# Two linear-attention layers on one core: the attention-output matrix from split factors in three float32r passes

## Chip, cores, metric

The kernel runs on one core of a Trainium2 chip. The metric is the device time of one execution in microseconds, as the median of several runs. One further execution was recorded by the hardware profiler; all lines of the trace come from it.

## What is computed

Two pairs of a linear-attention block A and a feed-forward block B, with the same weights in both pairs, on x of 2048 rows and 640 columns (32 heads of 20 columns, 1728 hidden units), all in float32:

```python
def _A_ref(x, wqkv, wo):
    qkv = (x @ wqkv).reshape(B, S, 3, H, Dh).transpose(2, 0, 3, 1, 4)
    q, k, v = qkv[0], qkv[1], qkv[2]
    phi = lambda t: jnp.where(t > 0, t + 1, jnp.exp(t)) + 1e-6
    pq, pk = phi(q), phi(k)
    kv = jnp.einsum("bhsd,bhse->bhde", pk, v)
    z = jnp.einsum("bhsd->bhd", pk)
    num = jnp.einsum("bhqd,bhde->bhqe", pq, kv)
    den = jnp.einsum("bhqd,bhd->bhq", pq, z)[..., None] + 1e-6
    return (num / den).transpose(0, 2, 1, 3).reshape(B, S, D) @ wo

def _B_ref(x, w1, b1, w2, b2):
    r = relu(einsum("bsd,df->bsf", x, w1) + b1)
    return einsum("bsf,fd->bsd", r * r, w2) + b2

x = x + _A_ref(_layernorm(x), A_wqkv, A_wo)
x = x + _B_ref(_layernorm(x), B_w1, B_b1, B_w2, B_b2)
...                                   # and both once more
```

## The kernel before

The 2048 rows are 16 tiles of 128 (`NT`), in four groups of four (`TG`). Large products are made in float32r, a form of float32 that TensorE takes in one pass with fewer bits. To keep the precision, each operand is split into a high part (a copy rounded to float32r, by ACT) and a low part (the operand minus the high part, by VectorE), and a product is the sum of three passes: low x high, high x low, high x high (`split`, `mm3`).

**Phase A, the loop over t.** For each tile, K and Q are projected (`part`), phi is applied (`Phi`: an exponential on ACT, L616, then two VectorE operations, L623 and L624), and x and phi(k) are split (`xh`, L925 and L955; `kh`, L810 and L820 in `k_post`). The products x^T phi(k) of the previous tile go into five PSUM banks (`g_part`, G) and, for pairs of tiles, into GT (`gt_part`). The sum of phi(k) over tiles is kept in `acc`: GpSimd adds the tiles with accumulating DMAs, and the last tile with an addition (L817). The q parts of six tiles in each layer are "late" (`LATE`): they are made after the loop by `late_q`, one half tile each.

**Between A and B.** This is the stretch that the change touches, in the order of the code:

1. Two late q parts (`late_q(2)`). Then a matrix of ones times `acc` sums phi(k) over the partitions, in two float32 matmuls of 320 columns (L1030); ACT copies it to `zbc`, with which VectorE makes the denominators (`b_ops`, walked through by `b_step`, `b_den`, `b_blocks`).
2. The last `g_part` and `gt_part`, and a transposition of GT into `Gs`.
3. `kv_make(c)` for six chunks of six heads (120 rows, the last one 40): G times the v weights, masked by VectorE to the block diagonal `kvbd` (L1084). v weights were loaded by `load_vo(0..2)`.
4. `m_make(c)` for the six chunks: kvbd times the rows of wo that belong to these heads, two float32 matmuls of 320 columns (L1093). The product, evicted by ACT (L1099) and moved into place by DMAs (L1103, L1105), is the attention-output matrix M, of 640 x 640; `m_split` splits its five chunks (L1108, L1109). The attention of a tile is then phi(q) / den times M: no per-head product is left.
5. The first products with M (`proj`, L538), for tiles 0 to 3, and the residual sums and norms that follow (`b_x1`); `b_load_x` loads x for them. Between all these steps `run_side` lets ACT move 32 x 32 blocks (L475) for transposed tiles.

The rest is the feed-forward block (`fc1`, `fc2_step`), with the attention of later groups woven in; the change does not touch it.

**Order and waits.** The order of instructions on each engine is the order in the code; each engine, and each DMA queue, takes them one after the other and waits at an instruction whose operands or whose tile aren't free. Tiles come from tagged rings: `f` (8 tiles of 128 x 640), `g` (5), `u` (6 tiles of twice that size), `r` (3, only for phase A). A new tile takes the buffer that was given up first, and its first writer waits for the last reader of the buffer. The loads of wo are issued by SyncE in the last two iterations of the loop:

```python
        if t >= 13:
            b_load_pq(t - 13)
            load_vo(2 * t - 26)
            load_vo(2 * t - 25)
```

PSUM has eight banks. `xbank` hands out banks 0, 1, 2 in turn, `kv_make` takes 3, 4, 5, 6, 7, 2, and `m_make` pairs from 4, 6, 2.

Of the kernel before, what the change touches and what calls it, by code (L numbers as in the profile page):

```python
# [31 lines left out]
HR = 6 * DH  # L32
# [21 lines left out]
F_BUFS, X_BUFS = 8, 5  # L54
# [14 lines left out]
def head_rows(c):  # L69
    return min(HR, D - HR * c)  # L70
# [3 lines left out]
def kernel(  # L74
# [11 lines left out]
    nc = tc.nc  # L86
# [5 lines left out]
    tmp = ctx.enter_context(tc.tile_pool(name="tmp", bufs=3))  # L92
# [26 lines left out]
    def ftile(name):  # L119
        return tmp.tile([P, D], F32, tag="f", name=name, bufs=F_BUFS)  # L120

    def gtile(name):
        return tmp.tile([P, D], F32, tag="g", name=name, bufs=X_BUFS)


    def split(hi, lo, src):

        nc.scalar.activation(hi, src, AF.Copy)
        nc.vector.tensor_tensor(out=lo, in0=src, in1=hi.bitcast(F32), op=ALU.subtract)
# [24 lines left out]
    def utile(name):  # L154
        return tmp.tile([P, 2 * D], R32, tag="u", name=name, bufs=RING)
# [86 lines left out]
    for m in ORDER:  # L242
        for k in range(PAIRS):
            a, b = unit_range(k)
# [310 lines left out]
    def a_stats(t):  # L555
        if t < NT:
            ln_stats(("a", t), xt[t])
# [12 lines left out]
    for layer in range(N_LAYERS):  # L570
# [57 lines left out]
        def rtile():  # L628
            return ap.tile([P, D], F32, tag="r", name="r", bufs=3)
# [28 lines left out]
        if layer == 0:  # L658
# [38 lines left out]
            first_loads.step(1, 5)  # L697
            first_loads.high(1)
            first_loads.low(1)
        ones = ap.tile([P, P], F32, name="ones", tag="ones", bufs=1)  # L700
        nc.gpsimd.memset(ones, 1.0)
        mask = ap.tile([HR, 6, DH], F32, name="mask", tag="mask", bufs=1)
        nc.gpsimd.memset(mask, 1.0)

# [9 lines left out]
        vo = {}  # L714

        def load_vo(i):

            u = utile("uraw").bitcast(F32).rearrange("p (j n) -> p j n", j=2)
            for j in range(2):
                c = 2 * (i % 3) + j  # L720
                if i < 3 and c < DC:
                    nc.sync.dma_start(u[:, j], wqkv[c * P : (c + 1) * P, 2 * D :])
                if i >= 3:
                    n = head_rows(c)
                    nc.sync.dma_start(u[:n, j], wo[c * HR : c * HR + n, :])
                vo["v" if i < 3 else "o", c] = u[:, j]

        pq, xr, pT, yzp, yzx, xn = {}, {}, {}, {}, {}, {}
        dens, xTb = {}, {}
# [15 lines left out]
        def b_load_x(t):  # L745
            xr[t] = x1_at(t)
            nc.sync.dma_start(xr[t], src[t])
# [59 lines left out]
        def k_post(t, r, between=()):  # L807

            kh[t] = u = xtile("kh")
            nc.scalar.activation(u[:, 0], r, AF.Copy)  # L810
            if t == 0:
                nc.gpsimd.tensor_copy(acc, r)
            else:
                if t < NT - 1:
                    nc.gpsimd.dma_start(acc, r, accum_op=ALU.add)
                else:
                    nc.gpsimd.tensor_tensor(out=acc, in0=acc, in1=r, op=ALU.add)  # L817
            for f in between:
                f()
            nc.vector.tensor_tensor(out=u[:, 1], in0=r, in1=u[:, 0].bitcast(F32), op=ALU.subtract)  # L820
# [32 lines left out]
        for t in range(NT):  # L853
# [117 lines left out]
            else:  # L971
                ps = part(t, 1024, 2 * D, bank(xb[2]))
                gs(1)
            k_post(t, f.r, [lambda: a_stats(t + 3)])
            if gt and not is_late:
                gt_part(t // 2 - 1, 1, bank(xb[1]))
            prep_step(t, 3)
# [43 lines left out]
        def run_keep(n):  # L1021
            for _ in range(min(n, len(keeps))):
                keep_kq(*keeps.pop(0))

        run_keep(2)
        late_q(2)
        zbc = tmp.tile([P, D], F32, tag="z", name="zbc", bufs=1)
        psz = [xbank()[:, :HD] for _ in range(2)]
        for j in range(2):
            nc.tensor.matmul(psz[j], ones, acc[:, j * HD : (j + 1) * HD], start=True, stop=True)  # L1030
        for j in range(2):
            nc.scalar.activation(zbc[:, j * HD : (j + 1) * HD], psz[j], AF.Copy)
        b_den(0)
# [32 lines left out]
        u = xtile("kvbd", F32).rearrange("p j n -> p (j n)")  # L1066
        kvbd = [u[:, HR * c : HR * (c + 1)] for c in range(NH)]
        maskf = mask.rearrange("p h d -> p (h d)")
        kvb = [3, 4, 5, 6, 7, 2]

        def kv_make(c):
            n = head_rows(c)
            kvb.append(kvb.pop(0))
            ps = bank(kvb[-1])

            o, m = HR * c, max(min(DM - HR * c, n), 0)
            parts = [v for v in ((0, m, G, o), (m, n, Gs, max(o - DM, 0))) if v[0] < v[1]]
            for q0, q1, g, w0 in parts:
                for d in range(DC):
                    nc.tensor.matmul(  # L1080
                        ps[:n, q0:q1], vo["v", d][:, o : o + n],
                        g[:, d, w0 : w0 + q1 - q0], start=d == 0, stop=d == DC - 1,
                    )
            nc.vector.tensor_tensor(out=kvbd[c][:n, :n], in0=ps[:n, :n], in1=maskf[:n, :n], op=ALU.mult)  # L1084

        mb = [4, 6, 2]

        def m_make(c):
            mb.append(mb.pop(0))
            ps = bank(mb[-1], 2)  # L1090
            n, o = head_rows(c), HR * c
            for j in range(2):
                nc.tensor.matmul(  # L1093
                    ps[:n, j * 512 : j * 512 + HD], kvbd[c][:n, :n],
                    vo["o", c][:n, j * HD : (j + 1) * HD], start=True, stop=True,
                )

            u = m_raw[0] if c == 0 else ftile("Mc")
            nc.scalar.activation(halves_sb(u[:n]), halves(ps[:n]), AF.Copy)  # L1099
            if c > 0:  # L1100
                m, r = divmod(o, P)
                k = min(P - r, n)
                nc.sync.dma_start(m_raw[m][r : r + k], u[:k])  # L1103
                if k < n:
                    nc.sync.dma_start(m_raw[m + 1][: n - k], u[k:n])  # L1105
# [7 lines left out]
        for c in range(NH):  # L1113
            kv_make(c)
            if c == 0:
                b_load_pq(3)
            if c == 1:
                b_load_x(0)
            if c == 3:
                b_load_x(1)  # L1120
            if c == 2:
                run_side(1)
            if c < 3:
                b_step(2)
        sg.close()
        sm = ExitStack()
# [10 lines left out]
        xbanks = [0, 1]  # L1137
        for c in range(NH):
            m_make(c)
            run_side(1)  # L1140
            b_step(3)
            if c == 2:
                late_q(1)
            if c in (3, 4):
                m_split(c - 3)
# [649 lines left out]
```

## Time and profile before

| | |
|---|---|
| median of 3 runs | 1312.54 us (1312.44 to 1313.02) |
| the profiled execution | 1313.91 us |
| its span, first to last instruction | 1312.2 us |
| granted TensorE clock | 1.0 |
| PE / VectorE / ACT / GpSimd busy | 1305.5 / 924.0 / 743.6 / 238.0 us |
| bytes moved | 339.94 MB, mean 259 GB/s |

Engines are called PE (TensorE matmuls), PEld (its weight loads), DVE (VectorE), ACT (ScalarE), POOL (GpSimd) and SP (SyncE, which issues most DMAs); a q behind the name is the engine's queue of DMA issues and waits. In a line of the timeline, the start (us from the start of the span) comes first, then the length of the burst, the engine, the line of the code, the operation, output <- inputs, shapes, and the number of instructions; in brackets at its end stands the engine's idle time before it and what ended that. In a line of groups the total busy time and the mean of one (ns) stand behind the bar. A profile that shows PE busy all the time says that PE never ran out of matmuls, not that each was fast.

### The profile page before, as it was taken

Reading aid. Unit: us, or ns where it says so; the run is one execution under the profiler, and the core shown is the slowest. Engines: PE = TensorE matmul, PEld = TensorE weight load, DVE = VectorE, ACT = ScalarE, POOL = GpSimd, SP = SyncE. Lnnn points to the kernel's source line nnn. Section 1 sums busy time; section 2 is a strip of 40 time slices with the busy share of each in tenths; the row PEclk is TensorE's granted clock in tenths of the full one; section 3 lists DMA queues with packets and bytes.
Section 4 is the critical chain, followed back from the end, with each engine's and each line's share of the span. In section 5 each row is a group of like instructions: output and inputs, shape, how many; then the busy total and the mean of one; then the engine's idle time right before and its main releaser. Section 6 shows DMA issues by size and latency. Waiting matters only on the chain.

```text
span 1312.2 us, 21124 instructions
## 1 busy us (share of the span) xinstructions
PE 1305.5 (99%) x7441; PEld 1187.8 (91%) x7441; DVE 924.0 (70%) x1697; ACT 743.6 (57%) x1636; POOL 238.0 (18%) x305
## 2 busy tenths in 40 slices
PE   9999999999999999999999999999999999999998
PEld 8888889989988988998988889999899899889888
DVE  7888978767865965833856677587779479579145
ACT  5888957785385476334322233387755934944242
POOL 2334310064032102101012222102330030021000
PEclk9999999999999999999999999999999999999999
DMA  6888985699996996998954456544879779779756
GB/s 194 249 278 268 310 256 167 248 353 386 304 342 207 307 344 231 290 369 293 354 173 125 126 141 170 146 175 169 328 275 372 274 257 326 294 253 313 288 187 221
DMA packets 143071, 339.94 MB, mean 259 GB/s; under 512 B 17318, under 2 KB 67622, under 8 KB 142326
## 3 DMA queue, kind: packets, MB, share of 16 engines
q1 hardware_dynamic: 135734, 316.31, 70.5%
q0 software_dynamic: 7232, 22.29, 6.6%
q8 instruction: 59, 0.97, 0.3%
q14 instruction: 46, 0.38, 0.1%
HBM read 255.92 MB, written 70.78 MB: 249 GB/s over the span
## 4 chain that ended last, share of the span: by engine, by line
PE 92%; DMA 3%; DVE 3%; SPq 1%; ACT 0%; issue 0%; POOL 0%; ACTq 0%; DVEq 0%
PE PS L1245 28%; PE PS L1328 24%; PE PS L603 18%; PE PS L511 11%; PE PS L1539 4%; PE PS L538 3%; PE PS L652 2%; DMA u<-kept 2%; PE PS L1080 1%; PE PS L1093 1%; DMA kept<-uprep 1%; PE PS L876 0%; DMA st<-in_B_w_dram 0%; DMA st<-in_A_wqkv_dram 0%; DVE uprep L332 0%
## 5 line engine op out<-in xcount | busy, mean ns | idle before, releaser
L1245 PE MATMUL PS<-xTb,u 128*128 128x512 f32 x1640 | 378.9, 390 | 0.0
L1245 PEld LDWEIGHTS PS<-xTb,u 128*128 128x128 f32 x1640 | 306.3, 188 | 61.9
L603 PE MATMUL PS<-kq,xT 128*128 128x320 f32 (+2 forms) x1575 | 283.9, 334 | 0.5 <-DVE r L624 0.4
L603 PEld LDWEIGHTS PS<-kq,xT 128*128 128x128 f32 x1575 | 250.3, 188 | 28.0 <-issue 1.2
L1328 PE MATMUL PS<-u,arena 128*128 128x320 f32 x1644 | 251.1, 309 | 0.7 <-DMA u<-kept 0.7
L1328 PEld LDWEIGHTS PS<-u,arena 128*128 128x128 f32 x1644 | 243.4, 188 | 1.6 <-issue 1.2
L475 ACT ACTIVATE z<-y 32x160 f32<-32x160 f32 x512 | 171.7, 335 | 41.5 <-DVE y L466 35.6
L1309 DVE TENSOR_TENSOR arena<-R,arena 128x512 fp32r<-128x512 f32 (+1 forms) x200 | 135.4, 683 | 82.1 <-ACT arena L1300 81.7
L1300 ACT ACTIVATE arena<-R 128x512 fp32r<-128x512 f32 (+1 forms) x200 | 116.2, 593 | 130.3 <-PE PS L1328 96.0
L1256 ACT ACTIVATE R<-PS,b1sb 128x512 f32<-128x512 f32 x104 | 71.5, 687 | 115.1 <-PE PS L1245 114.2
L511 PE MATMUL PS<-kh,xh 128*128 128x512 f32 x480 | 124.3, 393 | 0.0
L402 POOL TENSOR_SCALAR rs<-mv 128x1 f32<-128x1 f32 x64 | 32.5, 508 | 473.6 <-DVE mv L400 472.9
L1328 PE MATMUL PS<-uw,arena 128*128 128x320 f32 x660 | 106.1, 309 | 0.0
L511 PEld LDWEIGHTS PS<-kh,xh 128*128 128x128 f32 x480 | 87.3, 188 | 15.2 <-DVE xT L527 0.2
L1328 PEld LDWEIGHTS PS<-uw,arena 128*128 128x128 f32 x660 | 99.2, 188 | 0.4 <-DVE x L1342 0.2
L1274 DVE TENSOR_TENSOR R<-R 128x512 f32<-128x512 f32 (+1 forms) x128 | 88.8, 697 | 14.9 <-ACT R L1257 14.9
L499 ACT ACTIVATE z<-y 32x160 f32<-32x160 f32 x260 | 87.2, 335 | 3.1
L616 ACT ACTIVATE r<-PS 128x512 f32<-128x512 f32 (+1 forms) x64 | 27.7, 435 | 97.5 <-PE PS L603 96.3
L1257 ACT ACTIVATE R<-R 128x512 f32<-128x512 f32 x104 | 65.9, 634 | 3.3
L1342 DVE TENSOR_TENSOR x<-PS,x 128x320 f32<-128x320 f32 x112 | 53.2, 486 | 20.0 <-PE PS L1328 19.3
L623 DVE TENSOR_SCALAR r<-r 128x512 f32<-128x512 f32 (+1 forms) x64 | 21.3, 332 | 64.7 <-ACT r L616 64.6
L1550 DVE TENSOR_TENSOR x<-PS,x 128x320 f32<-128x320 f32 x48 | 23.2, 489 | 45.4 <-PE PS L1539 44.7
(156 smaller groups left out, 1552.1 us busy)
## 6 DMA issues: line engine op xcount, KB each, us to landing
u<-kept SPq DMA_DIRECT2D x113, 640.0 KB, 6.0
u<-kept_w SPq DMA_DIRECT2D x104, 640.0 KB, 6.3
u<-kept SPq DMA_DIRECT2D x56, 320.0 KB, 7.0
kept<-uprep SPq DMA_DIRECT2D x49, 320.0 KB, 5.2
z<-xb SPq DMA_DIRECT2D x160, 80.0 KB, 5.0
u<-kept_m SPq DMA_DIRECT2D x18, 640.0 KB, 5.5
pqt<-pq SPq DMA_DIRECT2D x32, 320.0 KB, 6.6
acc<-r POOLq DMA_DIRECT2D x28, 320.0 KB, 5.3
```

The costliest lines, as they stand in the source:

```text
L475: nc.scalar.activation(zv[j * B32 : (j + 1) * B32, :, i, :], yv[i * B32 : (i + 1) * B32, :, j, :], AF.Copy)
L499: nc.scalar.activation(dst, blk, AF.Copy)
L511: nc.tensor.matmul(ps, a, b, start=first and i == 0, stop=last and i == 2)
L603: nc.tensor.matmul(ps, xT[t][:, k, c, :], kq[c][:, l, a:b], start=(k, c, l) == seq[0], stop=(k, c, l) == seq[-1],)
L1245: nc.tensor.matmul(ps, a[:, d, :], bb[:, d, :], start=(d, i) == order[0], stop=(d, i) == order[-1],)
L1256: nc.scalar.activation(r, v, AF.Relu, bias=b1sb[:, c : c + 1])
L1257: nc.scalar.activation(r, r, AF.Square)
L1274: nc.vector.tensor_tensor(out=quad(*out, k), in0=quad(*x, k), in1=quad(*y, k), op=op)
L1300: nc.scalar.activation(u[:, 0], v, AF.Copy)
L1309: nc.vector.tensor_tensor(out=u[:, 1], in0=v, in1=u[:, 0].bitcast(F32), op=ALU.subtract)
L1328: nc.tensor.matmul(ps, x, y, start=opens and k == 0 and p == 0 and e == 0, stop=k == PAIRS - 1 and p == b - a - 1 and e == len(seq) - 1, s ...
L1342: nc.vector.tensor_tensor(out=v, in0=ps, in1=v, op=ALU.add)
```

## The change

In both layers:

- `m_make` for the five full chunks takes three float32r passes (high part of kvbd x low part of wo, low x high, high x high) for each half instead of one float32 matmul. The sixth chunk stays as it was.
- The sum of phi(k) is made in two float32r passes for each half, from `accl` and `acch`, the parts of `acc`. The ones are float32r now, made through a tile of the `r` ring.
- `kv_make` splits kvbd: after the masking of each full chunk, VectorE copies the high part and subtracts it (`kvs`, two tiles of the `r` ring).
- wo is split: its chunks 0 to 4 are loaded into `f` tiles (chunk 5 into a `g` tile), ACT makes the high parts in the `u` tiles that held wo before, and VectorE the low parts, in `g` tiles (the last of them in a `u` tile). `wo_split(0)` runs in the last iteration of the loop, `wo_split(1)` and `wo_split(2)` after it, ahead of `late_q(2)`.
- As the `g` tiles are taken until `m_make` has read them, the loads of x for tiles 0 and 1 move from `kv_make` into `m_make`; the `b_step(2)` calls move from chunks 0 to 2 of `kv_make` to chunks 3 to 5.

```diff
-        ones = ap.tile([P, P], F32, name="ones", tag="ones", bufs=1)
-        nc.gpsimd.memset(ones, 1.0)
+        ones = ap.tile([P, P], R32, name="ones", tag="ones", bufs=1)
+        one = rtile()[:, :P]
+        nc.gpsimd.memset(one, 1.0)
+        nc.gpsimd.tensor_copy(ones, one)
...
         def load_vo(i):
-            u = utile("uraw").bitcast(F32).rearrange("p (j n) -> p j n", j=2)
+            if i < 3:
+                u = utile("uraw").bitcast(F32).rearrange("p (j n) -> p j n", j=2)
+                for c in range(2 * i, min(2 * i + 2, DC)):
+                    nc.sync.dma_start(u[:, c % 2], wqkv[c * P : (c + 1) * P, 2 * D :])
+                    vo["v", c] = u[:, c % 2]
+                return
+            u = utile("uo").rearrange("p (j n) -> p j n", j=2)
             for j in range(2):
...
+                c = 2 * (i - 3) + j
+                vo["o", c] = raw = ftile("wo") if c < DC else gtile("wo")
+                n = head_rows(c)
+                nc.sync.dma_start(raw[:n], wo[c * HR : c * HR + n, :])
+                if c < DC:
+                    vo["hi", c] = u[:, j]
+                    vo["lo", c] = u[:, 1] if c == DC - 1 else tmp.tile([P, D], R32, tag="g", name="wl", bufs=X_BUFS)
+
+        def wo_split(i):
+            cs = range(2 * i, min(2 * i + 2, DC))
+            for c in cs:
+                nc.scalar.activation(vo["hi", c][:HR], vo["o", c][:HR], AF.Copy)
+            for c in cs:
+                nc.vector.tensor_tensor(
+                    out=vo["lo", c][:HR], in0=vo["o", c][:HR], in1=vo["hi", c][:HR].bitcast(F32), op=ALU.subtract
+                )
...
             k_post(t, f.r, [lambda: a_stats(t + 3)])
+            if t == NT - 1:
+                wo_split(0)
...
         run_keep(2)
+        wo_split(1)
+        wo_split(2)
+        acch, accl = (ap.tile([P, D], R32, tag="r", name="accs", bufs=3) for _ in range(2))
+        split(acch, accl, acc)
         late_q(2)
...
         for j in range(2):
-            nc.tensor.matmul(psz[j], ones, acc[:, j * HD : (j + 1) * HD], start=True, stop=True)
+            for i, a in enumerate((accl, acch)):
+                nc.tensor.matmul(psz[j], ones, a[:, j * HD : (j + 1) * HD], start=i == 0, stop=i == 1)
...
+        kvs = [ap.tile([P, D], R32, tag="r", name="kvs", bufs=3) for _ in range(2)]
...
             nc.vector.tensor_tensor(out=kvbd[c][:n, :n], in0=ps[:n, :n], in1=maskf[:n, :n], op=ALU.mult)
+            if c < DC:
+                h, l = (v[:n, o : o + n] for v in kvs)
+                nc.vector.tensor_copy(h, kvbd[c][:n, :n])
+                nc.vector.tensor_tensor(out=l, in0=kvbd[c][:n, :n], in1=h.bitcast(F32), op=ALU.subtract)
...
+            h, l = (v[:n, o : o + n] for v in kvs)
+            if c < DC:
+                seq = [(h, vo["lo", c]), (l, vo["hi", c]), (h, vo["hi", c])]
+            else:
+                seq = [(kvbd[c][:n, :n], vo["o", c])]
             for j in range(2):
...
+                for i, (a, w) in enumerate(seq):
+                    nc.tensor.matmul(
+                        ps[:n, j * 512 : j * 512 + HD], a, w[:n, j * HD : (j + 1) * HD],
+                        start=i == 0, stop=i == len(seq) - 1,
+                    )
...
-            if c == 1:
-                b_load_x(0)
-            if c == 3:
-                b_load_x(1)
             if c == 2:
                 run_side(1)
-            if c < 3:
+            if c >= 3:
                 b_step(2)
...
             m_make(c)
+            if c in (1, 3):
+                b_load_x(c // 2)
             run_side(1)
```

More of the change, by code (lines that the diff above doesn't have):

```diff
@@ L716, in load_vo @@
         def load_vo(i):
-            u = utile("uraw").bitcast(F32).rearrange("p (j n) -> p j n", j=2)
-            for j in range(2):
[L720 to L726, printed above, removed]
+            if i < 3:
[5 more added lines that the diff above has]
+            u = utile("uo").rearrange("p (j n) -> p j n", j=2)
+            for j in range(2):
+                c = 2 * (i - 3) + j
[13 more added lines that the diff above has]
+                )
         pq, xr, pT, yzp, yzx, xn = {}, {}, {}, {}, {}, {}
@@ L1091, in m_make @@
             n, o = head_rows(c), HR * c
-            for j in range(2):
[L1093 to L1096, printed above, removed]
+            h, l = (v[:n, o : o + n] for v in kvs)
[3 more added lines that the diff above has]
+                seq = [(kvbd[c][:n, :n], vo["o", c])]
+            for j in range(2):
+                for i, (a, w) in enumerate(seq):
[3 more added lines that the diff above has]
+                    )
             u = m_raw[0] if c == 0 else ftile("Mc")
```

## The prediction

> **What bounds the kernel now.** I read the page's busy times and its chain first, then the timeline of each engine around the lines that change.
>
> ```profile
> PE 1305.5 (99%) x7441; PEld 1187.8 (91%) x7441; DVE 924.0 (70%) x1697; ACT 743.6 (57%) x1636; POOL 238.0 (18%) x305
> ...
> PE 92%; DMA 3%; DVE 3%; SPq 1%; ACT 0%; issue 0%; POOL 0%; ACTq 0%; DVEq 0%
> ```
>
> TensorE (PE) is busy 1305.5 of the 1312.2 us span, and 92% of the chain that ended last is its own work. So a shorter PE step shortens the kernel only if PE then finds its next operands ready, and whatever makes PE wait is paid in full. All else is to be judged by one question: at which moments do VectorE (DVE), ScalarE (ACT) or a transfer come within a microsecond of being late for PE?
>
> The timeline of PE in layer 0 (columns: start us, length us, engine, line, operation, shape, count) around the sum of phi(k) (L1030) and the matrix M (L1093):
>
> ```profile
> 188.04 4.56 PE L603 MATMUL PS<-kq,xT 128*128 128x320 f32 x30
> 192.44 1.24 PE L1030 MATMUL PS<-acc,ones 128*128 128x320 f32 x4
> 193.27 3.85 PE L511 MATMUL PS<-kh,xh 128*128 128x512 f32 x15
> ...
> 210.63 3.39 PE L1093 MATMUL PS<-uraw,kvbd 120*120 120x320 f32 x12
> ...
> 224.02 13.48 PE L538 MATMUL PS<-uM,pT 128*128 128x320 f32 x90
> ```
>
> No idle time stands behind any of them: PE runs through. Layer 1 is the same stretch 649.47 us later (192.44 becomes 841.91), so I cost layer 0 and double it:
>
> ```profile
> 841.91 1.24 PE L1030 MATMUL PS<-acc,ones 128*128 128x320 f32 x4
> ```
>
> **Part 1: what PE saves.** The records of a burst overlap, so the pace is the burst less one record, over the count less one. One record of L1093 is modelled at 432 ns:
>
> ```profile
> L1093 PE MATMUL PS<-uraw,kvbd 120*120 120x320 f32 x40 | 11.4, 432 | 0.0
> ```
>
> A float32 record of 320 columns thus takes (3.39 - 0.43) / 11 = 0.269 us, and each float32 matmul is two records (the 40 are 20 matmuls of the five full chunks in two layers): 0.54 us. A float32r matmul of 320 columns is one record: from 188.04 to 192.44 are 30 of them, 0.147 us each. Three passes are 0.44 us, so each of the 10 matmuls of a layer saves 0.10 us: 0.97 us for M. The sum of phi(k) goes from four records to four passes: 4 x (0.269 - 0.147) = 0.49 us. That is 1.46 us a layer, 2.9 us in all, and it is the most that can be gained. By the page "FP8 and Floating Point Precision" of the Trainium skill (section TensorE Precision Notes), true FP32 makes four passes through the array; by four times 0.147 us a float32 matmul would be 0.59 us, and the saving 1.47 + 0.59 = 2.1 us a layer. The trace has 0.54 us, not 0.59 us, and decides.
>
> **Part 2: the sum of phi(k).** Before, L1030 needs only `acc`. After, it needs `accl`, which VectorE makes last in this order: five subtractions of wo (`wo_split`), then `accl`, and only then the two operations of the first late q part, L623 and L624, whose PSUM bank the second half of L1030 takes over (`xbank` turns over three banks; two late parts and two halves ask for four). The timeline of VectorE there:
>
> ```profile
> 186.05 0.82 DVE L955 TENSOR_TENSOR xh<-xt,xh 128x640 fp32r<-128x640 f32 x1
> 186.95 0.82 DVE L820 TENSOR_TENSOR kh<-r,kh 128x640 fp32r<-128x640 f32 x1
> 190.90 1.23 DVE L623 TENSOR_SCALAR rl<-rl 128x320 f32<-128x320 f32 x1 [3.13 <-ACT rl L616]
> 192.17 0.49 DVE L624 SCALAR_TENSOR_TENSOR rl<-PS,rl 128x320 f32<-128x320 f32 x1
> 193.10 0.33 DVE L623 TENSOR_SCALAR rl<-rl 128x320 f32<-128x320 f32 x1 [0.44 <-ACT rl L616]
> ```
>
> Two prices are read from rows of a later stage of VectorE and ACT, which part 4 uses too:
>
> ```profile
> 218.49 0.33 DVE L623 TENSOR_SCALAR rl<-rl 128x320 f32<-128x320 f32 x1 [2.56 <-ACT rl L616]
> ...
> 222.04 0.82 DVE L129 TENSOR_TENSOR pT<-z,pT 128x640 fp32r<-128x640 f32 x1 [0.71 <-ACT pT L128]
> 222.78 0.48 DVE L1108 CAST uM<-Mr 128x640 fp32r<-128x640 f32 x1
> ...
> 225.50 0.82 DVE L1109 TENSOR_TENSOR uM<-Mr,uM 128x640 fp32r<-128x640 f32 x1
> ```
> ```profile
> 211.91 0.70 ACT L1099 ACTIVATE Mr<-PS 120x640 f32<-120x640 f32 x1 [0.64 <-PE PS L1093]
> ```
>
> VectorE's 3.13 us of idle time before 190.90 look like a cover. They are not enough. A subtraction of 640 columns takes 0.82 us and hands over to the next after 0.74 us (222.04 to 222.78). From the end of L820 at 187.77 five of them and `accl` reach 187.7 + 5 x 0.74 + 0.82 = 192.2; L623 and L624 add 0.85 us (0.33 and 0.49 with a gap): 193.1.
>
> Then there is GpSimd's last addition to `acc`, in layer 0 and in layer 1:
>
> ```profile
> 190.37 1.58 POOL L817 TENSOR_TENSOR acc<-acc,r 128x640 f32<-128x640 f32 x1 [8.66 <-DMA acc<-r]
> ```
> ```profile
> 836.66 2.03 POOL L817 TENSOR_TENSOR acc<-acc,r 128x640 f32<-128x640 f32 x1 [8.24 <-DMA acc<-r]
> ```
>
> In layer 0 the 0.33 us operation L623 that met it took 1.23 us and ended just after it (192.13 and 191.95); in layer 1, where it began inside L820 (186.95 + 649.47 = 836.42), it took 2.03 us itself. Two-input subtractions suffer the same, as a row of the FFN shows, beside what the form takes on average:
>
> ```profile
> 536.37 2.09 DVE L1274 TENSOR_TENSOR R<-R 128x512 f32<-128x512 f32 x1
> ```
> ```profile
> 536.30 3.59 POOL L1225 TENSOR_TENSOR x<-x,b2bc 128x640 f32<-128x640 f32 x2
> ```
> ```profile
> L1274 DVE TENSOR_TENSOR R<-R 128x512 f32<-128x512 f32 x96 | 73.2, 763 | 14.9 <-ACT R L1257 14.9
> ```
>
> 2.09 us against 0.76 us, while GpSimd added: VectorE stood for 1.3 us. So somewhere between L820 and `accl` VectorE now loses about 1.4 us (1.58 us at the most) to L817, which before fell into its idle time. The page "SBUF — State Buffer" of the Trainium skill (section SBUF: two separate sides) makes a rule of it: a GpSimd operation and a VectorE operation with two SBUF inputs exclude each other, for the whole instruction. By this rule the loss is all of L817, without it nothing; the 2.09 us agree with it.
>
> A hand-over between engines takes about 0.2 us: the first four records of L1093 end at 210.63 + 4 x 0.269 = 211.71, and ACT's eviction L1099 starts at 211.91. So without the collision the second half of L1030 starts at 193.3 and ends two passes later at 193.6; before, the four records ended at 192.44 + 4 x 0.269 = 193.52. The saving of 0.49 us is gone: +0.1 us, the lower bound. With the collision it is +1.5 to +1.7 us, the upper. VectorE has no idle time left there to hide L817 in; layer 1, where L820 already took 0.6 us of it, is the row I stay near: +1.4 us a layer. PE's whole queue, L511 first, stands behind this wait.
>
> **Part 3: the loads of wo.** The raw chunks move from the `u` ring into `f` tiles, of which there are 8. In the last iteration (t = 15) the live ones are pqt 0 to 2, xt[15] and wo 0 to 3; so chunk 4 waits until xt[15] is read for the last time, which is L955: 186.87. SyncE, which issued all of this early, stands there with chunk 5 and, in layer 0, the stores of kq behind it:
>
> ```profile
> 174.38 2.60 SPq L725 DMA_DIRECT2D uraw<-in_A_wo_dram x4
> 178.50 2.47 SPq L204 DMA_DIRECT2D kept_kq<-kq x2
> ...
> 197.89 2.06 SPq L747 DMA_DIRECT2D x<-in_A_x_dram x2
> ```
>
> Those stores have time. Chunk 4 doesn't: ACT and VectorE take operations in order, and `acch`, `accl` and the late q parts stand behind it. How long do 300 KB take? The DMA issues (KB each, us to landing), and one stretch of layer 1:
>
> ```profile
> x<-in_A_x_dram SPq DMA_DIRECT2D x16, 320.0 KB, 5.8
> ...
> uraw<-in_A_wo_dram SPq DMA_DIRECT2D x10, 300.0 KB, 10.1
> ...
> Mr<-Mc SPq DMA_DIRECT2D x2, 280.0 KB, 3.0
> ```
> ```profile
> x<-x SPq DMA_DIRECT2D x2, 320.0 KB, 3.4
> ```
>
> From 3.0 to 10.1 us. The 10.1 us stand in a full queue; with the kq stores and two chunks of wo held back, about 1.7 MB fewer (two stores of 640 KB, 400 KB of wo) are in flight at 187, so I take 3.4 us: landed at 190.3, split by ACT (0.70 us, as L1099) by 191.1. VectorE comes to this chunk at 187.7 + 4 x 0.74 + 1.45 = 192.1, so up to 4.4 us cost nothing; each further microsecond is one for PE. At 10.1 us it would be 5.7 us more. No gain is possible here: before, nothing waited for wo.
>
> **Part 4: M.** After each of five `kv_make` VectorE gets a copy and a subtraction of 120 columns. At 640 columns they take 0.48 and 0.82 us (L1108, L1109); scaled by columns with a fixed part kept, about 0.2 + 0.27 us, 2.5 us a layer. The bounds are 1.2 us (by columns alone) and 6.5 us (as at 640 columns, which would be 3.2 us over the cover); I stay near the lower, as the operations are short. Cover is in the rows at 218.49 and 222.04: 2.56 + 0.71 us of idle time, so 2.5 us fit; that `b_step(2)` moves behind the later chunks changes the order, not the sum. But the 0.97 us saved on L1093 lead nowhere. The first product with M starts at 224.02; its 17th matmul (sixth of the third chunk of M, low part) is due at 224.02 + 16 x 0.147 = 226.37, and the low part is written at 225.50 + 0.82 = 226.32. PE is already level with this chain, which from 211.91 on is ACT's evictions and moves end to end and takes as long as before. It only starts 2 x 0.10 = 0.2 us sooner, with the first chunk of L1093. So M gives -0.2 us instead of -0.97 us. The two x loads, moved from 197.89 into this stage, cost SyncE 1.03 us each between the pieces of M and add transfers; `xr` is read only behind the first product with M: I take 0, at most half an issue, +0.5 us a layer. GpSimd's extra copy for `ones` is done long before: 0.
>
> **Sum.** +1.4 - 0.2 = +1.2 us a layer, +2.4 us. The profiled execution took 1313.91 us (span 1312.2 us), 1.37 us above the median of 1312.54 us; it becomes 1316.3 us, the median 1314.9 us. The dead zone of a measurement of this kernel is about 0.2%, 2.6 us: the forecast ends just inside it.
>
> **Rivals.** (a) Chunk 4 of wo lands late and takes the place as the last wait. For it: wo's own row says 10.1 us; against it: the queue should be empty by 187. It decides from 4.4 us on; at 5.8 us it adds 1.4 us a layer (1317.7), at 10.1 us 5.7 us (1326). Chance 0.34. (b) Not slower: L817 meets no subtraction, because `acc<-r` lands while VectorE waits for chunk 4; then +0.1 - 0.2 us a layer are left, 1312.3. For it: it did fall into idle time in layer 0; against it: `accl` needs it, so it cannot move behind. Chance 0.18. (c) The whole saving shows, 1309.6: M's third chunk would have to come 0.8 us sooner, and nothing in its chain gets shorter. Chance 0.06. The forecast keeps 0.42, half of it above the dead zone by tenths that I can't resolve (gaps, the x loads).
>
> **Numbers.** Slower by over 0.2%: 0.34 + 0.21 = 0.55; within: 0.21 + 0.18 = 0.39; faster: 0.06. Range 1311.9 to 1319.5: it takes in (b), the forecast and (a) up to about 6.7 us of landing; left out are (c) and the slowest third of (a).
>
> **What would show it.** Right: PE idle before L1030's passes, released by VectorE, over 1 us in each layer; L817 or a subtraction of wo stretched by over 1 us; VectorE without idle time from 186 to 194; chunk 4 issued just after L955; a wait of about 0.8 us for L1109 in the first product with M. Wrong: L1030 starting at its old distance from L603, or the first product with M starting without a wait.

## The result, and the profile after

| | before | after |
|---|---|---|
| median of 6 runs each | 1312.57 us (1312.44 to 1313.02) | 1317.93 us (1317.37 to 1319.42) |
| ratio, 95% interval | 1 | 1.0039 [1.0028, 1.0049] |
| span of the profiled execution | 1312.2 us | 1315.7 us |

The change makes the kernel slower by 5.4 us, 0.4%. Busy times and chain of the page after:

```profile
PE 1305.8 (99%) x7461; PEld 1188.8 (90%) x7461; DVE 939.1 (71%) x1729; ACT 749.4 (57%) x1648; POOL 240.1 (18%) x307
...
PE 88%; DVE 6%; ACT 3%; DMA 2%; issue 1%; SPq 1%; POOL 0%; DVEq 0%; ACTq 0%
```

PE's busy sum is the same as before, but the share of VectorE and ACT in the chain went from 3% to 9%: PE now waits for them. To see where, I took the starts of PE's records in both traces and compared stretch by stretch (after minus before, us). The first boundary lies behind L511, at the start of L652, since in the kernel before the first record of L511 overlaps the end of L1030:

| stretch of PE | layer 0 | layer 1 | forecast |
|---|---|---|---|
| late q parts, sum of phi(k) and L511, up to L652 | +1.26 | +1.11 | +1.4 |
| L652 to the first matmul of M | 0.00 | 0.00 | 0 |
| M to the first product with M | -0.75 | -0.74 | with the next row -0.2 |
| first product with M (90 matmuls) | +1.82 | +1.76 | |
| up to the feed-forward block | -0.03 | -0.02 | 0 |
| sum | +2.30 | +2.11 | +1.2 |

The two layers hold 4.4 of the 5.4 us. The two profiled spans differ by 3.5 us only: after, PE comes 0.3 us sooner to the first stretch (187.72 against 188.04), and before, it stood 0.54 us for a load in the feed-forward block (at 346.70) where after it does not stand. The profiled execution of before took 1.3 us more than its median and that of after 0.5 us less, so about a microsecond between the medians has no place in one stretch of these traces.

**The sum of phi(k).** PE, VectorE and GpSimd in layer 0 after:

```profile
187.72 4.56 PE L603 MATMUL PS<-kq,xT 128*128 128x320 f32 x30
193.30 0.55 PE L1054 MATMUL PS<-accs,ones 128*128 128x320 f32 x2 [1.03 <-DVE accs L129]
194.06 0.56 PE L1054 MATMUL PS<-accs,ones 128*128 128x320 f32 x2 [0.21 <-DVE rl L624]
```
```profile
186.62 0.82 DVE L837 TENSOR_TENSOR kh<-r,kh 128x640 fp32r<-128x640 f32 x1
187.36 4.41 DVE L741 TENSOR_TENSOR wl<-wo,uo 120x640 fp32r<-120x640 f32 x4
191.69 0.81 DVE L741 TENSOR_TENSOR uo<-wo,uo 120x640 fp32r<-120x640 f32 x1
192.43 0.81 DVE L129 TENSOR_TENSOR accs<-acc,accs 128x640 fp32r<-128x640 f32 x1
193.16 0.31 DVE L623 TENSOR_SCALAR rl<-rl 128x320 f32<-128x320 f32 x1
193.51 0.49 DVE L624 SCALAR_TENSOR_TENSOR rl<-PS,rl 128x320 f32<-128x320 f32 x1
```
```profile
186.63 2.25 POOL L834 TENSOR_TENSOR acc<-acc,r 128x640 f32<-128x640 f32 x1 [5.26 <-DVE xh L972]
```

VectorE has no idle time between 186.62 and 194.00. PE waits 1.03 us for `accl` (the tile `accs`) and 0.21 us for the bank that L624 reads. GpSimd's addition (L817 before, L834 now) falls among the subtractions of wo: four of them take 4.41 us. In layer 1 it met the subtraction of kh instead, 2.04 us where 0.82 us is usual, and the four subtractions ran undisturbed in 3.02 us:

```profile
837.96 2.04 DVE L837 TENSOR_TENSOR kh<-r,kh 128x640 fp32r<-128x640 f32 x1
839.92 3.02 DVE L741 TENSOR_TENSOR wl<-wo,uo 120x640 fp32r<-120x640 f32 x4
```

**M and the first product with it.** M leaves PSUM in chunks (evictions, by ACT), and each chunk but the first is moved into place by one or two DMAs, called its pieces here. Before, in layer 0 (VectorE, SyncE's queue, ACT):

```profile
211.30 0.33 DVE L623 TENSOR_SCALAR rl<-rl 128x320 f32<-128x320 f32 x1
```
```profile
212.18 0.33 SPq L1017 DMA_DIRECT2D pq<-rl  x1
214.48 0.78 SPq L1103 DMA_DIRECT2D Mr<-Mc  x1
```
```profile
218.41 0.70 ACT L1099 ACTIVATE Mc<-PS 120x640 f32<-120x640 f32 x1
```

After, SyncE, then ACT, VectorE and PE:

```profile
215.58 0.32 SPq L1036 DMA_DIRECT2D pq<-rl  x1
215.99 0.79 SPq L1138 DMA_DIRECT2D Mr<-Mc  x1
...
217.53 0.53 SPq L764 DMA_DIRECT2D x<-in_A_x_dram  x1
```
```profile
212.65 0.70 ACT L1134 ACTIVATE Mr<-PS 120x640 f32<-120x640 f32 x1 [0.45 <-PE PS L1128]
214.52 0.68 ACT L1134 ACTIVATE Mc<-PS 120x640 f32<-120x640 f32 x1
...
220.42 0.70 ACT L1134 ACTIVATE Mc<-PS 120x640 f32<-120x640 f32 x1 [1.23 <-DMA Mr<-Mc]
```
```profile
214.70 0.32 DVE L623 TENSOR_SCALAR rl<-rl 128x320 f32<-128x320 f32 x1
...
224.04 0.82 DVE L129 TENSOR_TENSOR pT<-z,pT 128x640 fp32r<-128x640 f32 x1 [1.97 <-ACT pT L128]
```
```profile
224.21 2.53 PE L538 MATMUL PS<-uM,pT 128*128 128x320 f32 x12
227.52 11.98 PE L538 MATMUL PS<-uM,pT 128*128 128x320 f32 x78 [0.78 <-DVE uM L1143]
```

The fourth eviction of M (chunk 3) writes the `f` tile that held chunk 1, and has to wait until the DMAs have moved chunk 1 into `Mr`. Before, ACT never waited for that: the late q part's store `pq<-rl` had gone out at 212.18, and the pieces of chunk 1 followed their eviction at once. After, VectorE comes to that late part 2.05 us behind the first eviction (214.70 against 212.65), where before it was 0.61 us ahead of it (211.30 against 211.91). So the store goes out at 215.58, the pieces behind it at 215.99 (evicted at 215.20), and the x load that the change put there at 217.53: 320 KB, 300 KB in two pieces and 320 KB within 2 us. ACT stands 1.23 us, VectorE 1.97 us for ACT, and PE for M's chunks.

### The profile page after: what moved, and what is told of

It reads as the page before. It is cut to its first block, busy times and chain, and to the rows that moved or that the text cites. A ratio compares the mean times of both kernels' runs of the same rounds, so it can differ in the third digit from the quotient of the medians.

```text
span 1315.7 us, 21220 instructions
## 1 busy us (share of the span) xinstructions
PE 1305.8 (99%) x7461; PEld 1188.8 (90%) x7461; DVE 939.1 (71%) x1729; ACT 749.4 (57%) x1648; POOL 240.1 (18%) x307
## 4 chain that ended last, share of the span: by engine, by line
PE 88%; DVE 6%; ACT 3%; DMA 2%; issue 1%; SPq 1%; POOL 0%; DVEq 0%; ACTq 0%
PE PS L1278 28%; PE PS L1361 26%; PE PS L603 15%; PE PS L511 10%; PE PS L1572 4%; PE PS L538 2%; PE PS L652 2%; ACT z L499 1%; ACT z L475 1%; DMA st<-in_B_w_dram 1%; PE PS L893 0%; DVE pqt L781 0%; DVE wl L741 0%; DMA kept<-uprep 0%; DMA st<-in_A_wqkv_dram 0%
## 5 line engine op out<-in xcount | busy, mean ns | idle before, releaser
L511 PE MATMUL PS<-kh,xh 128*128 128x512 f32 x480 | 123.8, 392 | 0.0
L511 PEld LDWEIGHTS PS<-kh,xh 128*128 128x128 f32 x480 | 87.2, 188 | 14.9 <-DVE xT L527 0.2
```

The source lines that it names most:

```text
L511: nc.tensor.matmul(ps, a, b, start=first and i == 0, stop=last and i == 2)
```

## The experiments

Theory on the first stretch: VectorE's new work ahead of `accl`, and GpSimd's addition in the middle of it, are late for PE. Rival: the load of wo's chunk 4 is. Theory on the product: ACT's wait for the pieces of M is what was missing from the sum. Rivals: VectorE's order, or the x loads alone. Each of the twelve kernels was timed against the kernel before on the same chip. The columns are the stretches of the table above, layer 0 / layer 1 (one number where the layers agree within 0.03 us):

| run | ratio [95%] | sum of phi(k) | M | first product |
|---|---|---|---|---|
| after | 1.0039 [1.0028, 1.0049] | +1.26 / +1.11 | -0.75 / -0.74 | +1.82 / +1.76 |
| e1 | 1.0049 [1.0036, 1.0063] | +1.47 / +1.27 | -0.73 | +1.59 / +1.77 |
| e2 | 1.0011 [1.0003, 1.0020] | -0.50 / -0.49 | -0.72 | +1.74 / +1.77 |
| e3 | 1.0025 [1.0015, 1.0035] | +1.27 / +1.10 | -0.76 | +1.09 / +1.02 |
| e4 | 1.0013 [1.0004, 1.0021] | +0.09 / +0.18 | -0.73 / -0.75 | +1.78 / +1.77 |
| e5 | 0.9992 [0.9984, 1.0001] | -0.49 / -0.50 | -0.70 | +0.91 / +0.72 |
| e6 | 1.0078 [1.0065, 1.0091] | -0.5 | -0.7 | +0.88 / +0.85 |
| e7 | 0.9991 [0.9982, 1.0000] | -0.50 / -0.49 | -0.71 / -0.70 | +0.56 / +0.49 |
| e8 | 1.0000 [0.9991, 1.0009] | +0.91 / -0.49 | none | none |
| e9 | 0.9986 [0.9977, 0.9994] | -0.49 / -0.50 | -0.70 / -0.69 | -0.11 / -0.11 |
| e10 | 1.0056 [1.0042, 1.0070] | +1.27 / +1.10 | -0.74 / -0.73 | +3.65 / +2.31 |
| e11 | 1.0030 [1.0019, 1.0041] | +1.27 / +1.09 | -0.74 / -0.73 | +1.49 / +1.49 |
| e12 | 1.0033 [1.0020, 1.0046] | +1.26 / +1.12 | -0.74 / -0.73 | +1.35 / +1.30 |

**e1: chunk 4 of wo loaded early**, into the unused half of the last v tile, so that its load waits for no `f` tile.

```
+                vo["spare"] = u[:, 1]
-                vo["o", c] = raw = ftile("wo") if c < DC else gtile("wo")
+                vo["o", c] = raw = vo["spare"] if c == DC - 1 else ftile("wo") if c < DC else gtile("wo")
```

> The changed kernel, but chunk 4 of wo is loaded into the unused half of the tile of the last v chunk, so its load no longer waits for the last read of xt[15] and lands some 8 us earlier. Theory (VectorE's chain of subtractions, lengthened by GpSimd's last addition, sets the wait before the sum of phi(k)): the wait of PE there stays at 1.0 + 0.2 us a layer, the time within 0.5 us of the changed kernel's 1317.9 us. Rival (the late load of chunk 4 sets it): the wait shrinks by the 0.8 us that ACT stands for that load, 1.6 us in both layers, 1316.3 us.

Nothing is gained: PE's wait stays. The addition now meets the subtraction of chunk 4 itself (2.20 us), which comes out of the early tile `uraw`:

```profile
190.45 2.20 DVE L742 TENSOR_TENSOR uo<-uraw,uo 120x640 fp32r<-120x640 f32 x1
```
```profile
190.19 1.78 POOL L835 TENSOR_TENSOR acc<-acc,r 128x640 f32<-128x640 f32 x1 [8.92 <-DMA acc<-r]
```

**e2: three of the five subtractions of wo behind the sum.** Chunks 0 and 1 are subtracted ahead of `accl`, the others behind `b_den(0)`; ACT makes the high parts of chunks 2 to 4 behind `acch`.

```
-        wo_split(1)
-        wo_split(2)
+        wo_low(range(2))
         split(acch, accl, acc)
...
         b_den(0)
+        wo_low(range(2, DC))
```

> The changed kernel, but of the splits of wo only the two subtractions of chunks 0 and 1 stay ahead of accl; the other three subtractions come behind the first denominators, where VectorE has 2.2 us of idle time, and ACT makes acch before the high parts of chunks 2 to 4. Theory: VectorE reaches accl 2.2 us sooner, PE no longer waits at the sum of phi(k), which then shows its two saved passes: -1.2 - 0.4 = -1.6 us a layer, 1314.6 us; the waits in the first product with M stay. Rival (what PE waits for there is not VectorE's queue but acc or the load): the wait stays, 1317.9 us.

PE runs through, and the stretch is 0.50 us shorter than before the change, the whole saving of part 1, though the addition still stretches two subtractions (2.93 us; the next two of the same kernel, undisturbed, take 1.55 us):

```profile
192.09 0.75 PE L1056 MATMUL PS<-accs,ones 128*128 128x320 f32 x4
```

**e4: without GpSimd's addition of tile 15 to acc.** The sum of phi(k) thus leaves out the last 128 rows.

```
-                else:
-                    nc.gpsimd.tensor_tensor(out=acc, in0=acc, in1=r, op=ALU.add)
```

> The changed kernel without GpSimd's addition of tile 15 to acc: the sum of phi(k) leaves out the last 128 rows. Theory (that addition stops VectorE for 1.4 us among the subtractions): VectorE's stretched subtraction goes back to 0.8 us, PE's wait before the sum of phi(k) falls by 1.2 us a layer, 1315.5 us. Rival (the five subtractions and accl alone are too long): at most 0.3 us a layer, 1317.3 us.

```profile
187.43 3.02 DVE L741 TENSOR_TENSOR wl<-wo,uo 120x640 fp32r<-120x640 f32 x4
```
```profile
192.28 1.23 PE L1052 MATMUL PS<-accs,ones 128*128 128x320 f32 x4
```

3.02 us for the same four subtractions, and +0.09 and +0.18 us are left of the stretch: the collision costs 1.2 and 0.9 us.

**e8: only the sum of phi(k) in two passes** (with the split of `acc` ahead of the late q parts), M and wo as before.

```
+            for i, a in enumerate((accl, acch)):
+                nc.tensor.matmul(psz[j], ones, a[:, j * HD : (j + 1) * HD], start=i == 0, stop=i == 1)
```

> The kernel before with one part of the change alone: the sum of phi(k) in two float32r passes from accl and acch; wo and M as before. Theory (two passes save 0.49 us where nothing is late): VectorE has only accl to make, GpSimd's addition falls into idle time, PE does not wait: -0.5 us a layer, 1311.6 us. Rival (acc itself comes too late for a split): PE waits, 1313 us or more.

The theory holds in layer 1 (no wait, -0.49 us) and not in layer 0: there VectorE is idle, and `acc` itself is late, since the addition starts only when the accumulating DMA has landed:

```profile
189.70 1.57 POOL L819 TENSOR_TENSOR acc<-acc,r 128x640 f32<-128x640 f32 x1 [8.98 <-DMA acc<-r]
```
```profile
192.95 0.56 PE L1035 MATMUL PS<-accs,ones 128*128 128x320 f32 x2 [0.67 <-DVE accs L129]
```

When this DMA lands in layer 0 goes with the kernel, as far as one profile of each can show: in the changed kernel and all its variants that keep the addition, e1 aside, SyncE stands with the load of chunk 4, and the addition starts at 186.3 to 188.3; in the kernel before, e8 and e1, where the loads of wo are out early, at 189.7 to 190.4. A fuller DMA queue would explain it; no run tests that alone.

**e3: the last `b_step(2)` behind the late q part** (`if 3 <= c < 5` for `if c >= 3`), so that VectorE comes to the late part sooner.

> The changed kernel, but the third b_step(2) of kv_make (1.4 us of VectorE) comes after the late q part that ends there instead of before it, so that part's store is issued 1.4 us sooner. Theory (SyncE stands with that store, the pieces of M queue behind it, their tiles come free late, and ACT stands 1.2 us before the fourth eviction of M): the pieces go out as soon as they are evicted, ACT's wait goes, PE's wait in the first product with M falls from 1.8 to 0.8 us a layer, 1315.9 us. Rival (the two x loads between the pieces on SyncE delay M): the wait stays, 1317.9 us.

```profile
214.34 0.32 SPq L1036 DMA_DIRECT2D pq<-rl  x1
215.36 0.78 SPq L1138 DMA_DIRECT2D Mr<-Mc  x1
```
```profile
219.81 0.70 ACT L1134 ACTIVATE Mc<-PS 120x640 f32<-120x640 f32 x1 [0.49 <-DMA Mr<-Mc]
```

The store goes out 1.24 us sooner, the pieces right behind their eviction, ACT's wait falls from 1.23 to 0.49 us, and the product loses 0.73 us less.

**e5: e2 and e3 together.**

> The changed kernel with both edits, three subtractions of wo behind the first denominators and the late q part's store ahead of the third b_step(2). Theory: the two waits are independent and the gains add: against before -0.5 us a layer at the sum of phi(k), -0.7 us at M, +1.05 us of waits in the first product with M (0.7 us less than in the changed kernel), so -0.2 us a layer, 1312.2 us. Rival (PE, coming 1.7 us sooner to M, finds the chain of M that much later): the waits grow and the time stays at 1314.6 us.

The two add up; the loss is gone.

**e6: e5, with the x loads behind chunks 3 and 5, `m_split(2)` ahead of a late q part, and ACT's `run_side` held back until chunk 2 of M.**

> As the kernel before it, with the x loads behind chunks 3 and 5 of m_make, and ACT makes the first three evictions of M without block moves between them, and the third chunk of M is split ahead of the last late q parts. Theory (what is left of the wait is ACT's order of moves and evictions): the chain of M comes over 2 us sooner, the first product with M hardly waits (at most +0.2 us), -1.1 us a layer, 1310.4 us. Rival (the moves only shift their delay to the attention of tile 1, whose split then comes late): the wait moves to the second product, 1312 us.

A miss. ACT no longer waits for the pieces, but the block moves that it put off come due all at once, and PE waits for them later; 6.9 us in layer 0 and 4.5 us in layer 1 are lost behind the first product:

```profile
241.80 6.20 PE L538 MATMUL PS<-uM,pT 128*128 128x320 f32 x30 [2.61 <-DVE pT L129]
...
260.40 1.89 PE L1282 MATMUL PS<-xTb,u 128*128 128x512 f32 x7 [2.51 <-ACT xTb L128]
```

Not all of it is waiting: the 30 matmuls at 241.80 take 6.20 us where they take 4.56 us before, as the granted TensorE clock falls to 0.5 behind the wait of 2.61 us (last section). ACT has no slack in this stretch, though its share of busy time is 57%.

**e7: e5, with the x loads behind chunks 3 and 5 of M.**

```
-            if c in (1, 3):
-                b_load_x(c // 2)
+            if c in (3, 5):
+                b_load_x((c - 3) // 2)
```

> The kernel with both edits, and the two x loads behind chunks 3 and 5 of m_make instead of 1 and 3. Theory (an x load issued right behind the pieces of chunk 1 shares the DMA engines with them, and ACT's fourth eviction waits 0.5 us for their tile): that wait goes, the waits in the first product with M fall to the 0.7 us that PE gains on ACT's chain, -0.5 us a layer against before, 1311.5 us. Rival (the x loads do not matter): 1312.2 us, and ACT's wait of 0.5 us stays.

```profile
211.10 0.71 ACT L1138 ACTIVATE Mr<-PS 120x640 f32<-120x640 f32 x1 [0.44 <-PE PS L1132]
...
217.64 0.71 ACT L1138 ACTIVATE Mc<-PS 120x640 f32<-120x640 f32 x1
```

ACT's wait is gone: 6.54 us from the first to the fourth eviction, 6.50 us before the change.

**e9: e7, with `m_split(2)` ahead of the late q part that stood before it on VectorE.**

> The kernel with the wo subtractions, the third b_step and the x loads moved (as in e7), and m_split(2) ahead of the next late q part instead of behind it. That kernel still lost 0.56 and 0.49 us a layer in the first product with M. Theory: what is left is VectorE's order (the rest of a late q part stands in front of the third chunk's copy and subtraction); then the product loses about 0.1 us a layer, the layer gains 1.1 us over the kernel before the change, the kernel 2.2 us: ratio 0.9983, against 0.9991 for e7. Rival: VectorE now stands in front of chunk 2's copy until the pieces of M have landed, and what is queued behind it (the late q rest, the split of tile 3) comes late by as much: 0.5 us a layer or more stay, in the first product or behind it; ratio 0.999 or above.

```profile
223.12 13.36 PE L538 MATMUL PS<-uM,pT 128*128 128x320 f32 x90
...
243.28 3.93 PE L603 MATMUL PS<-kq,xT 128*128 128x320 f32 x25 [0.19 <-DVE x L809]
```

The 90 matmuls run through (13.36 us, 13.48 us before the change), so what was left in e7 was VectorE's order. Of the 0.67 and 0.60 us that this gains in the product, 0.41 and 0.34 us come back just behind, where PE waits for the residual sum (L809): both theories are right in part. e9 is the fastest kernel here, 2.2 us under the kernel before on the same chip (1311.26 against 1313.47 us), though within the 0.2% named in the prediction.

**e10: the stores of the late q parts issued by GpSimd** (`nc.gpsimd.dma_start` for `nc.sync.dma_start`), the kernel otherwise as changed.

> The changed kernel with one edit: the store of a late q part (pq<-rl) is issued by GpSimd instead of SyncE; order and work of all else stay. Theory (SyncE stands with that store until VectorE has made the late part's rest, and the pieces of M queue behind it, so that their f tile is free late): ACT's wait of 1.23 us for Mr<-Mc before its fourth eviction of M falls below 0.5 us, the first product with M loses about 1.0 us instead of 1.8 (as in e3), the layer 1.3 to 1.5 us instead of 2.2: about 1316.4, ratio 1.0025. The stretch of the sum of phi(k) stays at +1.1 to +1.3 us. Rival: VectorE itself is late with the split of M's chunks, whatever SyncE does: the product still loses 1.7 us or more, and the time stays at ratio 1.004.

```profile
215.41 0.79 SPq L1138 DMA_DIRECT2D Mr<-Mc  x1
```
```profile
219.84 0.44 ACT L616 ACTIVATE rl<-PS 128x320 f32<-128x320 f32 x1 [0.93 <-DMA pq<-rl]
221.09 0.70 ACT L1134 ACTIVATE Mc<-PS 120x640 f32<-120x640 f32 x1 [0.81 <-DMA Mr<-Mc]
```

My theory as written there fails: with SyncE free of the store the pieces go out only 0.58 us sooner, and ACT still waits for them, and for the store besides. A queue that stands is at most a part of it; the bytes of the store move at the same time whoever issues it.

**e11: the store issued by SyncE behind the pieces of chunk 1**, the kernel otherwise as changed.

> The changed kernel with one edit: the store of the late q part that is made ahead of M (pq<-rl, SyncE) is issued behind the pieces of M's chunk 1 instead of ahead of them. VectorE's order and all data stay. In the changed kernel the store goes out at 215.58 and the pieces of chunk 1 at 215.99; letting GpSimd issue the store freed SyncE by 0.58 us only and left ACT's wait, as the 320 KB then moved among the pieces all the same. Theory (what the lateness of VectorE's late part costs is that the store stands ahead of the pieces, in SyncE's order and on the DMA engines): the pieces go out at 215.2, land about 2 us earlier, ACT's wait of 1.23 us for Mr<-Mc falls below 0.5 us, the first product with M loses about 1.0 us a layer instead of 1.8: ratio about 1.0025. Rival 1 (the x load of 320 KB behind the pieces is what makes them late): ACT's wait falls by less than 0.4 us. Rival 2 (VectorE's order alone): the product still loses 1.7 us or more even where ACT no longer waits.

```profile
219.35 0.44 ACT L616 ACTIVATE rl<-PS 128x320 f32<-128x320 f32 x1 [0.51 <-DMA Mr<-Mc]
220.20 0.70 ACT L1138 ACTIVATE Mc<-PS 120x640 f32<-120x640 f32 x1 [0.42 <-DMA pq<-rl]
```

Half a miss: the first wait shrinks to 0.51 us, and the store, late now, makes a second one. ACT's two waits together are only 0.3 us shorter than the one before, which is what rival 1 (the x load) had asked for; e12 tests it alone.

**e12: only the x loads moved**, as in e7, the kernel otherwise as changed.

> The changed kernel with one edit: the two x loads are issued behind chunks 3 and 5 of M instead of 1 and 3. Theory (store and pieces collide, the x load adds to it): ACT's wait for Mr<-Mc before its fourth eviction falls from 1.23 us to 0.6 to 0.9 us, the first product with M loses 1.2 to 1.5 us a layer instead of 1.8, ratio about 1.003. Rival 1 (the x load is the cause by itself): ACT's wait goes to below 0.3 us, the product loses 0.9 us or less, ratio about 1.002. Rival 2 (VectorE's order alone): nothing changes, ratio 1.004.

```profile
220.40 0.71 ACT L1134 ACTIVATE Mc<-PS 120x640 f32<-120x640 f32 x1 [0.76 <-PE PS L1128]
```

ACT waits 0.76 us (the profile names PE, whose matmuls of this chunk had long ended; the second piece of chunk 1 lands at 220.24), within the theory's 0.6 to 0.9 us, and the product loses 1.35 and 1.30 us.

**The runs together.** ACT's way from the first to the fourth eviction of M, against the 6.50 and 6.48 us before, and what the first product loses:

| run | ACT longer by, layer 0 / 1 | product loses | difference |
|---|---|---|---|
| after | 1.27 / 1.24 | 1.82 / 1.76 | 0.55 / 0.52 |
| e2 | 1.22 / 1.26 | 1.74 / 1.77 | 0.52 / 0.51 |
| e11 | 0.94 / 0.96 | 1.49 / 1.49 | 0.55 / 0.53 |
| e12 | 0.80 / 0.77 | 1.35 / 1.30 | 0.55 / 0.53 |
| e3 | 0.53 / 0.47 | 1.09 / 1.02 | 0.56 / 0.55 |
| e5 | 0.40 / 0.23 | 0.91 / 0.72 | 0.51 / 0.49 |
| e7 | 0.04 / -0.01 | 0.56 / 0.49 | 0.52 / 0.50 |
| e10 | 1.76 / 1.81 | 3.65 / 2.31 | 1.89 / 0.50 |

What ACT waits in this stretch PE waits in the product, one for one; e1 and e4 fit too (0.51 to 0.54 us), and layer 0 of e10 does not, for a reason of its own (last section). e6 is outside the rule: ACT's way is 0.5 us shorter there, and PE waits for `pT` in its place. The constant 0.5 us is the wait that part 4 of the prediction forecast: PE comes to the product 0.74 us sooner, the chain of M only 0.2 us. e9 takes it away, so it is VectorE's order. So the 1.8 us are 1.25 us of ACT's wait, to which the late q part with its store (0.7 us, e3) and the x load behind it (0.5 us, e12) add, and 0.5 us of the order on VectorE. What each of the store's two roles weighs, ahead of the pieces in SyncE's order and beside them on the DMA engines, is not separated: e10 and e11 each brought a new wait for the store.

## Why the prediction was right or wrong

The kernel is slower, as forecast, and 1317.93 us lies within the range of 1311.9 to 1319.5 us. That is luck in part: the forecast was 1314.9 us, and the upper half of the range was there for rival (a), a late load of wo's chunk 4, which did not come. What fills it is a wait that the sum left out.

- **Part 1 (PE's saving): right.** Where PE waits for nothing the sum of phi(k) is shorter by 0.49 to 0.50 us (e2, e5, e7, e9; 0.49 forecast). M is shorter by 0.74 us, not 0.97: its passes come at the forecast pace, but PE stops ahead of the fifth half (0.14 us, and the first pass behind the stop is 0.10 us longer). That half writes bank 2, which `kv_make` used last for its sixth chunk, and VectorE reads that bank (L1109) only until 213.42, behind the operations that the change put ahead of it; the trace names this L1109 as the releaser in both layers.

```profile
213.24 0.18 DVE L1109 TENSOR_TENSOR kvbd<-PS,mask 40x40 f32<-40x40 f32 x1
```
```profile
213.47 0.41 PE L1128 MATMUL PS<-wl,kvs 120*120 120x320 f32 x1
```

- **Part 2 (the sum of phi(k)): right**, by mechanism and size: +1.26 and +1.11 us for +1.4. The lower bound of +0.1 us, without the collision, is what e4 measured (+0.09, +0.18). The loss to GpSimd's addition is 1.39 us in layer 0 (4.41 against 3.02 us) and 1.22 us in layer 1 (2.04 against 0.82). By the rule of the Trainium skill's page "SBUF — State Buffer" (section SBUF: two separate sides) it would have been all of the addition's 1.58 us; the trace agrees in kind, and the measured loss is a little less.
- **Part 3 (the loads of wo): right.** Chunk 4 went out behind L972's read of xt[15] at 187.3, and ACT split it at 189.88 after a wait of 0.79 us, well before VectorE came to it at 191.69. That is 2.6 us from issue to use, where 3.4 us were taken. Rival (a) is out by e1.

```profile
189.88 0.74 ACT L739 ACTIVATE uo<-wo 120x640 fp32r<-120x640 f32 x1 [0.79 <-DMA wo<-in_A_wo_dram]
```

- **Part 4 (M): the step that failed.** Its own terms hold: the copy and the subtraction of kvbd take 0.22 and 0.28 us (0.2 and 0.27 forecast), and with ACT's wait gone, M and the product together gain 0.15 and 0.21 us (e7), for the 0.2 us forecast.

```profile
207.50 0.22 DVE L1112 CAST kvs<-kvbd 120x120 fp32r<-120x120 f32 x1
207.76 0.28 DVE L1113 TENSOR_TENSOR kvs<-kvbd,kvs 120x120 fp32r<-120x120 f32 x1
```

   What failed is the sentence on the order: that the moved `b_step(2)` "changes the order, not the sum". I matched 2.5 us of new VectorE work with 2.56 + 0.71 us of idle time, but that idle time lies behind the late q part, and the new work ahead of it. So the late part, its store and the pieces of M behind it came late, and the x load came on top. I priced SyncE's queue for the x loads only, at 0 to 0.5 us; the row of the store and the return of chunk 1's `f` tile were not in the sum at all. So M and the product came out at +1.07 and +1.02 us for -0.2. That is 1.25 us a layer, 2.5 us of the 3 us by which the forecast was short; part 2 came out 0.4 us cheaper in the two layers, and about 1 us is the part of the medians' difference that no stretch shows.
- **Rivals.** (b) had its price right and its condition wrong. (c), the whole saving, needed M's third chunk sooner; "nothing in its chain gets shorter" was too strong, since in e9 ACT's chain is as long as in e7 and the product still runs through: the last link, VectorE's order, could be shortened. Even there 0.4 us come back at the residual sum.
- **The signs named for "right"** nearly all showed, and did not reach the step that failed. The sign for the product, one wait of about 0.8 us, is in the trace (0.78 us), but for the copy L1143 and not for the subtraction behind it, and it is only part of the 1.8 us: the 12 matmuls ahead of it take 2.53 us where 12 at 0.147 us would take 1.9. The 17th matmul is the fifth of M's third chunk, not the sixth as the prediction says; its time is right, so nothing hangs on that.

## What to carry to other kernels

Idle time covers new work only if it lies ahead of the next thing that somebody waits for: match a new operation with the gap in front of the next store, load or eviction, not with the gaps of the stage. When a step is moved or delayed, follow what it issues to the end: a store that goes out later may move its bytes among other transfers, and the tile that these transfers were to give back comes late for an engine that never touched the step. And an engine of 57% busy time may have no slack in the one stretch that counts (e6).

## What the runs showed of the hardware that I had not expected

In e10's profiled execution PE's clock was halved for over 3 us in the first product of layer 0, behind two waits, of 0.55 and 0.77 us, that had left PE busy for 0.45 and 0.43 us of the microseconds in which they fall (columns: window, length, busy time and count of PE, PEld, DVE, ACT and POOL, clock, DMA share, GB/s):

```profile
225.00:226.00 1.00, 0.45 (x4) 0.19 (x2) 0.97 (x3) 0.98 (x4) 0.00 (x0) 1.00 0.78 271
226.00:227.00 1.00, 0.99 (x5) 0.73 (x6) 0.93 (x2) 0.96 (x4) 0.00 (x0) 1.00 0.41 102
227.00:228.00 1.00, 0.43 (x2) 0.16 (x2) 0.96 (x3) 0.96 (x4) 0.00 (x0) 1.00 0.59 151
228.00:229.00 1.00, 0.81 (x4) 0.64 (x4) 0.96 (x3) 0.95 (x3) 0.54 (x1) 0.84 0.81 207
229.00:230.00 1.00, 1.00 (x4) 0.95 (x4) 0.97 (x3) 0.96 (x4) 0.00 (x0) 0.50 0.67 182
```

That is why layer 0 lost 3.65 us there and layer 1, at full clock with the same waits, 2.31 us. The Trainium skill's page "TensorE: Matmul & The Clock Gate" (section Part 1: The HAM clock gate) gives half the clock after an idle window of about 3.4 us. Here PE was never idle for that long; the dip's depth agrees with the page, its condition is wider. In the changed kernel the waits of the same place are shorter in sum, and the clock stays at 1.0. In e6 the clock fell to 0.50 for 3.4 us in both layers, behind waits of 2.61 and 2.60 us, and cost 1.6 us more each time. So short waits can cost more than themselves.

Why layer 1 of e10 kept its clock with the same waits is not tested. One reading fits: the two drops in e6 start at 242.14 and 897.50, which is 192 times the 3.413 us that each lasts, as if the clock were set anew in a fixed raster of such windows. Counted from the drop in e10 (228.67), both waits of layer 0 lie in one window of the raster, and those of layer 1 in two.
